# Reordering the attention-by-value units and the global rows' output in a fused local/global attention and MLP kernel

## Chip, cores and metric

One core of one Trainium2 chip. The metric is the device time of one execution in microseconds, with the median of all runs given. The kernel before takes 308.43 us (median of three runs, 307.68 to 312.75). The span in a profile (first to last instruction) is some 1.7 us shorter than that run's device time.

## The reference, cut to what matters

Batch 8, 8 heads, head width 64. Each batch has 32 global tokens, which attend to everything, and 512 local tokens, which attend to the 32 global ones and to their neighbours within 32 positions. The attention output of all heads is the input of an MLP with a quick GELU.

```python
# q_l, k_l, v_l: (8, 8, 512, 64)   q_g, k_g, v_g: (8, 8, 32, 64)
s_g  = scale * q_g @ concat(k_g, k_l).T          # global rows see all 544 tokens
out_g = softmax(s_g) @ concat(v_g, v_l)
s_ll = where(|i - j| <= 32, scale * q_l @ k_l.T, -1e9)
s_l  = concat(scale * q_l @ k_g.T, s_ll)         # local rows: 32 global keys + the window
out_l = softmax(s_l) @ concat(v_g, v_l)
x = concat(out_g, out_l).transpose(0, 2, 1, 3).reshape(8 * 544, 512)
h = x @ w_in                                     # 512 -> 2048
g = h * sigmoid(1.702 * h)
return g @ w_out                                 # 2048 -> 512, float32, 4352 rows
```

## The kernel before: the parts concerned

A `Quad` is four heads of one batch, so each batch has a first and a second head group. Scores are computed with keys on the partitions. The product with the values ("AV") is done in three *units*: unit 0 multiplies by ones and gives the denominators, units 1 and 2 give the two halves of the head width. Each unit fills one PSUM bank (a part of the memory that matmuls write their sums into; copying a finished bank out is its *eviction*) in two steps: `ekU` adds the global keys' share (four 32-row matmuls), and `U` adds the local keys' share (16 matmuls). Line numbers `L...` in the profiles are those of the kernel that ran.

```python
def XK(self, two=True):                 # exp of the global keys' scores, bank kb -> ek   (L375)
    nc.scalar.activation(self.ek, self.kb, AF.Exp, scale=scale)
    self.ek2 = None
    if two:                             # a copy turned by 32 partitions, by two transfers
        load_turned(nc.sync, self.ek2, self.ek)

def ekU(self, unit, warm=0, ov=None):   # a unit's global keys                             (L392)
    if ov is None:
        ov = pbank("ov")                # one of four PSUM banks, reused in turn
    ...
    two = unit == 1 and self.ek2 is not None   # unit 1 on the turned row group, beside unit 0
    ...

def ekUs(self, nxt=None, rnd=0, banks=(None, None, None)):   # all three, with the next keys between
    ...

def R(self):    # denominators: transpose sT (L442), reciprocal rT (L444), transpose rs (L446)
def XL(self, h):                        # xL = unit 1 + h times rs: frees that unit's bank (L451)
    nc.vector.tensor_mul(self.x[:, 2 * self.u + h, :], self.st[1 + h], self.st["rs"])
def Gm(self, og=None): ...              # the global queries' rows                         (L436)
def G(self):                            # ... scaled and transposed into xG                (L459)
    ...
    nc.vector.transpose(xG[:, 2 * self.u : 2 * self.u + 2, Sg * self.b : Sg * self.b + Sg], ...)

def o_mm(i, st): ...                    # output projection, op, four matmuls a step       (L512)
def o_out(i, tci, op):
    ...
    nc.scalar.activation(ob[:, lo:hi], op[:, lo:hi], AF.Copy, scale=0.5)       # eviction  (L526)
    for j in range(4):
        eng = nc.scalar if last and j % 2 else nc.sync
        ...
            r = (4 * tci + j) * S       # global tokens: batch-major, 32 rows per transfer
            rows = out[r : r + Sg, :]
        eng.dma_start(out=rows[:, lo:hi], in_=ob[32 * j : 32 * j + 32, lo:hi])

# batch 0, second head group c
for unit in range(3):
    c.ekU(unit)
for unit in range(3):
    c.U(unit)
c.R()
...
# batch 1: first head group a, second c
    a.XK(False)                         # no turned copy
    ...
    c.S(1)
    a.ekUs(c, 1)
    c.X(1)                              # exp of the scores (L339), then
    c.XK(False)                         # exp of the global keys
    for unit in range(3):
        a.U(unit)
    ...
    pt = spair()                        # the four banks of the scores c.S(1)
    a.Gm(bank(pt, 0)[:, 0 : D + 2])
    osteps(0, (3, 0), (3, 1))           # eight output matmuls
# the last batch, second head group
    for f4 in range(3):
        o_mm(i, 8 + f4)
    for unit in range(3):
        c.ekU(unit)
        c.U(unit)
    o_mm(i, 11)
    c.Gm()
    c.RXG()                             # R, XL(0), XL(1), G
    o(3)                                # takes the next PSUM bank in turn
```

The softmax here doesn't subtract the row's maximum and nothing guards it: scores larger than these inputs give would overflow.

## Time and profile before

From batch 2's second half on, the tensor engine's work repeats rigidly: two runs, laid over each other there, agree within a few hundredths of a microsecond until the last batch. So the span can be cut at fixed instructions into stretches, and a change shows in the stretch where it acts. The cuts are starts of matmuls on the tensor engine (PE), except the last two.

| stretch | from, to | before, us |
|---|---|---|
| start-up | start, to the second head group's first unit of batch 0 | 16.65 |
| batch 0 | to that group's global rows (L436) | 5.99 |
| MLP 0 | to the end of batch 1's scores (L327, at 47.05) | 24.41 |
| batch 1 | to the next keys' matmuls (L327, at 51.27) | 4.22 |
| middle | to the last batch's first unit (253.86) | 202.59 |
| last batch | to the first projection matmul after it (L487) | 6.95 |
| MLP 7 and globals | to the end of the last eviction on ScalarE (ACT) | 42.14 |
| tail | to the end of the span | 3.11 |

The timeline of PE in the kernel before, at batch 0, at batch 1 and at the last batch (start, duration, engine, line, operation, output and inputs, count; in brackets the idle time just before and what ended it):

```profile
16.88 0.88 PE L392 MATMUL ov<-ek,rvg 32*32 32x512 bf16 x8
17.68 0.49 PE L418 MATMUL ov<-e,ones 128*32 128x160 bf16 x16
...
18.94 1.67 PE L487 MATMUL s<-xL,w_in_sb 128*128 128x512 bf16 x7 [0.16 <-DMA w_in_sb<-in_moe_w_in_dram]
20.82 1.89 PE L487 MATMUL s<-xL,w_in_sb 128*128 128x512 bf16 x8 [0.21 <-DVE xL L451]
...
49.45 1.89 PE L512 MATMUL op<-w_out_sb,gT 128*128 128x512 bf16 x7 [0.34 <-ACT ek L375]
...
257.34 1.90 PE L512 MATMUL op<-w_out_sb,gT 128*128 128x512 bf16 x8
```

In batch 0 the eight global matmuls of units 1 and 2 take 0.88 us as one group, because the third unit waits for its bank inside it; the local units can only follow at 17.68. A bracket counts from the end of the last matmul, but in a running group the matmuls overlap: the seven from 18.94 start 0.216 us apart and last 0.38 us each. The last line has no bracket: PE did not wait there. The same place on VectorE (DVE):

```profile
254.72 0.72 DVE L442 STREAM_TRANSPOSE sT<-ov 128x512 f32<-128x512 f32 x1 [0.87 <-PE ov L418]
...
256.58 1.29 DVE L451 TENSOR_TENSOR xL<-ov,rs 128x512 bf16<-128x512 f32 x2
```

Two multiplies `xL` in 1.29 us: the first takes 0.69 us.

ACT at batch 1 in the kernel before, scores first, then the global keys:

```profile
47.16 1.66 ACT L339 ACTIVATE e<-s 128x856 bf16<-128x856 f32 x2
48.71 0.20 ACT L341 ACTIVATE e<-s 128x32 bf16<-128x32 f32 x1
48.79 0.62 ACT L375 ACTIVATE ek<-kb 128x512 bf16<-128x512 f32 x1
```

### The profile page before, as it was taken

Reading aid. Unit: us, or ns where it says so; the run is one execution under the profiler, and the core shown is the slowest. Engines: PE = TensorE matmul, PEld = TensorE weight load, DVE = VectorE, ACT = ScalarE, POOL = GpSimd, SP = SyncE. Lnnn points to the kernel's source line nnn. Section 1 sums busy time; section 2 is a strip of 40 time slices with the busy share of each in tenths; the row PEclk is TensorE's granted clock in tenths of the full one; section 3 lists DMA queues with packets and bytes.
Section 4 is the critical chain, followed back from the end, with each engine's and each line's share of the span. In section 5 each row is a group of like instructions: output and inputs, shape, how many; then the busy total and the mean of one; then the engine's idle time right before and its main releaser. Section 6 shows DMA issues by size and latency. Waiting matters only on the chain.

```text
span 306.1 us, 7822 instructions
## 1 busy us (share of the span) xinstructions
PE 296.3 (97%) x3230; PEld 148.3 (48%) x3265; DVE 211.0 (69%) x446; ACT 169.3 (55%) x282; POOL 54.4 (18%) x86
## 2 busy tenths in 40 slices
PE   7899999999999999999999999999999999999995
PEld 6454445444454455445454455445454454446653
DVE  6668847978957876777867876777777855574320
ACT  4828485485556745565556655565456661673421
POOL 8542755540050001400050002100000000000000
PEclk9999999999999999999999999999999999999999
DMA  7999999999399122951299023901230021201122
GB/s 192 180 208 206 191 150 224 211 176 145 79 98 181 33 56 71 149 110 28 62 116 174 3 57 85 106 0 40 51 79 9 2 62 38 60 0 35 37 61 77
DMA packets 56100, 29.39 MB, mean 96 GB/s; under 512 B 42880, under 2 KB 45952, under 8 KB 56064
## 3 DMA queue, kind: packets, MB, share of 16 engines
q0 software_dynamic: 45696, 16.95, 49.9%
q1 hardware_dynamic: 9888, 11.29, 14.2%
q10 hardware_dynamic: 480, 0.66, 0.6%
q8 instruction: 25, 0.41, 0.6%
q14 instruction: 11, 0.09, 0.1%
HBM read 35.13 MB, written 8.91 MB: 144 GB/s over the span
## 4 chain that ended last, share of the span: by engine, by line
PE 91%; ACT 3%; DMA 2%; DVE 1%; issue 1%; SPq 0%; ACTq 0%
PE op L512 38%; PE hp L487 37%; PE s L308 6%; PE ov L418 5%; PE ov L392 2%; DMA q<-in_q_l_dram 2%; ACT e L339 1%; PE kb L327 1%; PE op L524 1%; PE s L487 1%; PE s L327 1%; PE s L436 1%; ACT e L336 1%; DVE xL L451 0%; ACT ob L526 0%
## 5 line engine op out<-in xcount | busy, mean ns | idle before, releaser
L512 PE MATMUL op<-w_out_sb,gT 128*128 128x512 bf16 x504 | 120.0, 380 | 1.9 <-issue 0.5
L495 DVE SCALAR_TENSOR_TENSOR gT<-th,hp 128x512 bf16<-128x512 f32 (+1 forms) x140 | 91.2, 656 | 41.8 <-ACT th L494 40.7
L487 PE MATMUL hp<-xL,w_in_sb 128*128 128x512 bf16 x487 | 108.4, 379 | 0.6
L494 ACT ACTIVATE th<-hp 128x512 f32<-128x512 f32 (+1 forms) x140 | 79.8, 573 | 43.2 <-PE hp L487 39.7
L487 PEld LDWEIGHTS <-w_in_sb 128*128 128x128 bf16 x576 | 56.2, 98 | 64.8 <-issue 1.1
L512 PEld LDWEIGHTS <-gT 128*128 128x128 bf16 x528 | 49.3, 98 | 56.6 <-issue 3.8
L339 ACT ACTIVATE e<-s 128x856 bf16<-128x856 f32 x62 | 51.4, 882 | 12.1 <-PE s L436 7.0
L526 ACT ACTIVATE ob<-op 128x512 f32<-128x512 f32 (+2 forms) x35 | 20.5, 585 | 59.0 <-PE op L512 56.5
L89 POOL DMA_DIRECT2D v<-in_v_l_dram x24 | 18.7, 782 | 112.8 <-PE s L436 107.8
L442 DVE STREAM_TRANSPOSE sT<-ov 128x512 f32<-128x512 f32 x15 | 10.8, 717 | 27.1 <-PE ov L418 27.1
L346 DVE TENSOR_TENSOR e<-e,mask 128x1408 bf16<-128x1408 bf16 x28 | 24.4, 870 | 5.5 <-ACT e L339 5.5
L308 PE MATMUL s<-q,kT 32*128 32x228 bf16 (+5 forms) x528 | 21.2, 280 | 1.1 <-DVE q L269 1.1
L451 DVE TENSOR_TENSOR xL<-ov,rs 128x512 bf16<-128x512 f32 x30 | 19.4, 686 | 2.2 <-PE ov L418 0.9
L308 PEld LDWEIGHTS <-kT 32*128 32x128 bf16 x528 | 11.0, 95 | 14.9 <-issue 6.6
L265 DVE STREAM_TRANSPOSE kT<-rk 128x512 f32<-128x512 f32 (+1 forms) x17 | 16.9, 994 | 1.1 <-DMA rk<-in_k_l_dram 1.1
L375 ACT ACTIVATE ek<-kb 128x512 bf16<-128x512 f32 x16 | 9.7, 606 | 9.6 <-PE kb L327 9.6
L418 PE MATMUL ov<-e,v 128*32 128x160 bf16 (+1 forms) x480 | 12.1, 239 | 0.0
L446 DVE STREAM_TRANSPOSE rs<-rT 128x512 f32<-128x512 f32 x16 | 11.4, 711 | 0.6
L269 DVE STREAM_TRANSPOSE q<-rq 128x512 f32<-128x512 f32 (+1 forms) x17 | 10.9, 640 | 0.8 <-ACT rq L550 0.8
L418 PEld LDWEIGHTS <-v 128*32 128x32 bf16 x512 | 10.0, 97 | 0.9 <-issue 0.9
L327 PE MATMUL kb<-q,kgT 32*32 32x512 bf16 x128 | 10.1, 387 | 0.0
L487 PE MATMUL hp<-xG,w_in_sb 128*128 128x256 bf16 x64 | 9.6, 273 | 0.1
(80 smaller groups left out, 167.4 us busy)
## 6 DMA issues: line engine op xcount, KB each, us to landing
out_dram<-ob SPq DMA_DIRECT2D x132, 64.0 KB, 1.7
v<-in_v_l_dram POOLq DMA_DIRECT2D x32, 128.0 KB, 6.6
rq<-in_q_l_dram POOLq DMA_DIRECT2D x6, 512.0 KB, 8.7
rk<-in_k_l_dram POOLq DMA_DIRECT2D x6, 512.0 KB, 10.9
w_out_sb<-in_moe_w_out_dram POOLq DMA_DIRECT2D x4, 512.0 KB, 11.5
ek<-ek SPq DMA_DIRECT2D x12, 96.0 KB, 3.0
w_in_sb<-in_moe_w_in_dram POOLq DMA_DIRECT2D x4, 256.0 KB, 9.8
w_in_sb<-in_moe_w_in_dram POOLq DMA_DIRECT2D x2, 512.0 KB, 13.1
```

The costliest lines, as they stand in the source:

```text
L89: nc.gpsimd.dma_start(out=vtiles[b % 2][p, s, :, :, :D], in_=vf[b, g][:, hs])
L265: nc.vector.transpose(self.kT.rearrange("p (r t) -> p t r", t=16)[:, lo:hi], loaded[self.b][0][:, self.u].bitcast(F32)[:, 32 * lo : 32 * hi])
L308: nc.tensor.matmul(ps[j][:, off : off + n], lhsT=self.k[p, 128 * c : 128 * c + 128, e], rhs=self.q[p, lo:hi, r0 : r0 + nr, e], start=(e == ...
L339: nc.scalar.activation(e[:, 2 * i : 2 * i + 2, :RW], self.ps[i][:, :, :RW], AF.Exp, scale=scale)
L346: nc.vector.tensor_mul(e, e, mask[:, rnd : rnd + 1, :].to_broadcast([128, 4, LW]))
L418: nc.tensor.matmul(ov[32 * j : 32 * j + 32, :].rearrange("p (t r) -> p t r", t=16)[:, :, r0 : r0 + nr], lhsT=lv, rhs=self.E[c // 2][:, j, ...
L451: nc.vector.tensor_mul(self.x[:, 2 * self.u + h, :], self.st[1 + h], self.st["rs"])
L487: nc.tensor.matmul(hp[:, : width(i)], lhsT=w_in_c[:, fc // 8, kc, fc % 8 // 2, :, fc % 2], rhs=(xL[i] if i < B else xG)[:, kc, :], start=( ...
L494: nc.scalar.activation(th[:, :n], hp[:, :n], AF.Tanh, scale=0.851)
L495: nc.vector.scalar_tensor_tensor(gTs[i][:, fc, :n], in0=th[:, :n], scalar=1.0, in1=hp[:, :n], op0=ALU.add, op1=ALU.mult)
L512: nc.tensor.matmul(op, lhsT=gTs[i][:, fc, tci * 128 : tci * 128 + 128], rhs=w_out_sb[:, fc, :], start=(first and fc == 4 * f4), stop=(fc = ...
L526: nc.scalar.activation(ob[:, lo:hi], op[:, lo:hi], AF.Copy, scale=0.5)
```

## The change

Its intent: take PE's short waits out of batches 0 and 1, pack the last batch's units as the middle batches have them, and write the global tokens' output with fewer transfers. To do the last, the columns of `xG` are ordered by query first and batch second, so 128 rows of the output tile are 16 queries of all 8 batches, and two engines write half the columns each.

```diff
-                xG[:, 2 * self.u : 2 * self.u + 2, Sg * self.b : Sg * self.b + Sg],
+                xG.rearrange("p k (s b) -> p k s b", b=B)[:, 2 * self.u : 2 * self.u + 2, :, self.b],
@@ o_out
+            if i == B:
+                rows = out.rearrange("(b t) m -> t b m", t=S)[16 * tci : 16 * tci + 16]
+                mid = (lo + hi) // 2
+                nc.sync.dma_start(out=rows[:, :, lo:mid], in_=ob[:, lo:mid])
+                nc.scalar.dma_start(out=rows[:, :, mid:hi], in_=ob[:, mid:hi])
+                continue
             for j in range(4):
...
@@ batch 0
-    for unit in range(3):
-        c.ekU(unit)
-    for unit in range(3):
-        c.U(unit)
+    c.ekU(0)
+    c.ekU(1)
+    c.U(0)
     c.R()
+    c.U(1)
+    c.ekU(2)
+    c.U(2)
@@ batch 1
+    load_turned(nc.sync, rvt[:, 2:4], rvg[:, 2:4])
...
-    a.XK(False)
+    a.XK()
...
+    c.XK(False)
     c.X(1)
-    c.XK(False)
@@ last batch
+            c.ekUs()
             for unit in range(3):
-                c.ekU(unit)
                 c.U(unit)
```

(The change came under a title that also named "global values of batch 0 as f32"; the prediction refers to it.)

More of the change, by code (lines that the diff above doesn't have):

```diff
@@ L526, in o_out @@
             nc.scalar.activation(ob[:, lo:hi], op[:, lo:hi], AF.Copy, scale=0.5)
-            for j in range(4):
-                eng = nc.scalar if last and j % 2 else nc.sync
-                if i < B:
-                    rows = out[i * S + Sg : (i + 1) * S, :].rearrange("(r t) m -> t r m", t=16)[4 * tci + j]
-                else:
-                    r = (4 * tci + j) * S
-                    rows = out[r : r + Sg, :]
-                eng.dma_start(out=rows[:, lo:hi], in_=ob[32 * j : 32 * j + 32, lo:hi])
+            if i == B:
[4 more added lines that the diff above has]
+                continue
+            for j in range(4):
+                rows = out[i * S + Sg : (i + 1) * S, :].rearrange("(r t) m -> t r m", t=16)[4 * tci + j]
+                nc.sync.dma_start(out=rows[:, lo:hi], in_=ob[32 * j : 32 * j + 32, lo:hi])
     def act4(i, hf):
```

## The prediction

> **What bounds the kernel now.** I read the page's busy line and chain first, then the waits of the tensor engine alone, then the timeline at each place the diff touches.
>
> ```profile
> PE 296.3 (97%) x3230; PEld 148.3 (48%) x3265; DVE 211.0 (69%) x446; ACT 169.3 (55%) x282; POOL 54.4 (18%) x86
> ...
> PE   7899999999999999999999999999999999999995
> ...
> DMA  7999999999399122951299023901230021201122
> ...
> PE 91%; ACT 3%; DMA 2%; DVE 1%; issue 1%; SPq 0%; ACTq 0%
> ```
>
> PE is busy 296.3 of 306.1 us and carries 91% of the chain that ended last. The change takes no matmul away and adds none (3230 before; the built program has the same number), so it can only win idle time and badly packed time of PE, plus the two ends. The DMA row matters as well: nearly all slices up to about 46 us (6 of 40) stand at 9.
>
> ```profile
> PE op L512 <- ACT ek L375: 0.3, 1, 0.3
> PE s L487 <- DVE xL L451: 0.2, 1, 0.2
> ```
>
> These are two of the rows of the waits view for PE; no row there exceeds 1.5 us, and that one is the start-up. They are the waits the change is aimed at: 0.21 us in batch 0 (at 20.82) and 0.34 us in batch 1 (at 49.45). A change that wins both whole wins 0.55 us, 0.2% of the time. A third place shows in the timeline of PE, the last batch, where the units of AV run one by one:
>
> ```profile
> 253.86 0.39 PE L392 MATMUL ov<-ek,ones 32*32 32x512 bf16 x4
> 254.18 0.49 PE L418 MATMUL ov<-e,ones 128*32 128x160 bf16 x16
> 254.60 0.40 PE L392 MATMUL ov<-ek,rvt 32*32 32x512 bf16 x4
> 254.93 0.49 PE L418 MATMUL ov<-e,v 128*32 128x160 bf16 x16
> 255.34 0.40 PE L392 MATMUL ov<-ek,rvg 32*32 32x512 bf16 x4
> 255.67 0.49 PE L418 MATMUL ov<-e,v 128*32 128x160 bf16 x16
> 256.32 0.81 PE L512 MATMUL op<-w_out_sb,gT 128*128 128x512 bf16 x3 [0.16 <-issue]
> ```
>
> From 253.86 to 256.32 is 2.46 us. The same work in a middle batch stands packed:
>
> ```profile
> 85.06 0.40 PE L392 MATMUL ov<-ek,rvt 32*32 32x512 bf16 x4
> ...
> 85.63 0.49 PE L418 MATMUL ov<-e,ones 128*32 128x160 bf16 x16
> 85.95 0.78 PE L418 MATMUL ov<-e,v 128*32 128x160 bf16 x32
> 86.56 0.30 PE L436 MATMUL s<-v,e 128*32 128x66 bf16 x16
> ```
>
> There all global units begin at 85.05, the local ones at 85.63, and the next work at 86.56: 1.51 us, although eight matmuls for the next keys are mixed in.
>
> **What the Trainium skill says.** (1) "Perfetto Trace Analysis", Identifying the Most-Contended Engine: matmul busy share is no measure of the distance to the roofline, since pipelined instructions look different in the trace. It agrees here: in the last batch PE looks busy for all but 0.16 us of 2.46, yet the same work takes 1.51 elsewhere. (2) "TensorE: Matmul & The Clock Gate", Part 3: matmuls on different 32-row tiles run at once. It agrees: four 32x512 matmuls of 0.39 us each advance the chain by 0.33, and with values on a turned row group two units start 0.01 us apart (85.05 and 85.06). (3) "DMA: Bandwidth & Descriptors", Issuing engines are not separate DMA queues: transfers from all issuers interleave on the same 16 DMA engines. The trace agrees in landing times: an output write takes 1.7 us in the median of the whole kernel, 4.4 us when issued at 42 us among the loads. (4) Same page, Specifications: pieces under 512 B are below line rate. No line of before isolates it.
>
> **The change part by part.**
>
> *Global values of batch 0 as f32.* The title names it, but the diff has none of it; the kernel before already loads them so. 0.
>
> *Batch 0.* Before, the third global unit stands ahead of the first local one and waits for its bank until the multiply that ends at 17.31; local unit 0 starts at 17.68. After, it need not wait, so it starts near 17.25 (16.65 plus two global units) and the chain sT, rT, rs, eg, xL shifts by about 0.4 us; xL ends near 20.35 and PE needs it at 20.61. The wait of 0.21 goes. One more switch between global and local units costs perhaps 0.05. On PE: -0.15 to -0.2.
>
> *Does that last?* Not wholly. At 42 us DVE waits for a load, and PE's scores of batch 1 (44.04) follow directly:
>
> ```profile
> 42.23 1.05 DVE L265 STREAM_TRANSPOSE kT<-rk 128x512 f32<-128x512 f32 x1 [1.11 <-DMA rk<-in_k_l_dram]
> ...
> 43.73 0.42 DVE L279 COPY q<-qgT 128x40 f32<-128x40 f32 x4
> ```
>
> The first of these four copies ends near 43.9, so PE can come at most about 0.1 us earlier. And the change puts 49.5 KB (the turned values, rvt) and 128 KB (the turned exponentials, ek2) on the DMA engines in this crowded stretch. At some 190 GB/s, the page's rate there, 49.5 KB is 0.26 us; ek2 is issued only at 40.7. I put the delay of this load at 0.2 us. Batch 0 with this: +0.1.
>
> *Batch 1, turned values.* Packing as in the middle batches brings the local units from 47.85 to about 47.65 (0.80 us from the scores' end there, 0.63 in a middle batch): -0.2 if the data are there. ek2 needs its transfers landed at about 47.1. The exponential ends at 40.64, its two transfers are issued at 40.7 and 41.3. The like pair later:
>
> ```profile
> ek<-ek SPq DMA_DIRECT2D x1, 96.0 KB, 7.8
> ...
> ek<-ek SPq DMA_DIRECT2D x1, 32.0 KB, 7.5
> ```
>
> That was at 52 us, when output writes took 5.7 us; those issued at 42 us took 4.4. Scaled by 4.4/5.7 it is 6.0 and 5.8 us: landing at 46.7 and 47.1. A coin toss; I charge 0.2 us on average.
>
> *Batch 1, exp of global keys first.* The bank of kb is free sooner, so the 0.34 us wait goes. But the exp of the scores is now second on ACT, and the global-row matmuls (L436, 48.78 before) write into the pair of banks which that exp reads; in the built program they wait for its first half in both kernels. Before: the exp starts at 47.16 and its first half ends near 48.0, in time. After: kb is complete about 0.75 us after the scores (47.80, as 245.19 to 245.94 in a later batch), its exp takes 0.60, the first half of the other 0.86: 49.26. L436 starts at 49.3 instead of 48.78, and the output matmul at about 49.6 instead of 49.45: +0.15, and this swallows the packing's 0.2, which lies before the new wait. Batch 1 together: +0.35.
>
> *Last batch.* 253.86 + 0.58 (all global units, an upper bound since no next keys are mixed in) + 0.93 (local units) + 0.16 (switch) = 255.53 against 256.32: -0.8. ek2 already exists there, its bank waits are for an eviction that ended by 251.3, and what follows on DVE has over 2 us of slack. All of it is on PE's path and comes through to the end.
>
> *Global tokens in query-major order.* The little transposes (0.25 us each, off PE's path) write with a stride: at most 0.1 us each, hidden. The output goes in one transfer per queue instead of two:
>
> ```profile
> 301.71 0.38 ACTq L534
> ...
> 302.13 0.43 ACTq L534
> ...
> 302.61 0.33 ACT ob L526
> ```
>
> The second issue ends at 302.56 and the last matmul at 302.53, so the last eviction gains nothing. After it one issue of 0.43 instead of two: -0.4; but the transfer has 128 pieces of 384 B instead of 32 of 768 B, and issues with 96 rows took 0.53 to 0.61. I give half back: -0.2.
>
> Sum: +0.1 + 0.35 - 0.8 - 0.2 = -0.55 us.
>
> **The rivals.** (a) All aimed-at waits vanish and nothing takes their place: -0.2 - 0.5 - 0.8 - 0.4 = -1.9 us, about 306.5. For it: PE bound everywhere; against: the bank pair, fixed by the program's order. (b) ek2 or rvt lands late, since the DMA engines are full and the hardware queue shares with the loads: PE stands at the second global unit, and kb, both exps and L436 all move back with it, one for one. A landing 2 us later makes +1.5 us net, about 309.5. For it: 7.8 us of the like pair; against: 4.4 us of the writes at 42 us. (c) The strided small pieces at the end take longer than the saved issue: +0.5 us, 308.5. (d) The slow, unexplained executions (312.75 in the three runs of before) fall into the median: noise, not the change.
>
> **Range and chances.** Before: 308.43 in the median, 307.68 at best, and 307.79 in the profiled run; a typical run is thus near 308.2, and I take off 0.55: 307.6. Low 306.3 is rival (a) with a good draw; high 309.2 is (b) half true. 2% is 6.2 us, more than three times rival (a): faster 0.01, same 0.98, slower 0.01.
>
> **What would show it.** Right: the last batch's stretch shrinks to about 1.65 us; the wait of PE for xL is gone; PE shows a new wait at L436 near 49 us whose releaser is ACT; the ACT order there is ek before e. Wrong: a PE wait of over 0.5 us on the DMA of ek2 or rvt (rival b); L436 starts before 48.9 (my bank argument fell); the end of the last issue to the end of the span longer than in before by 0.4 us or more (rival c); DVE's wait for rk at 42 us unchanged (no extra load delay).

## The result

The changed kernel takes 308.37 us (median of six runs, 307.64 to 309.22); the kernel before took 308.19 in the median of its six. The ratio of the changed kernel to the one before is 1.0012, with a 95% interval of 0.9991 to 1.0034. Of the six of the kernel before, one (312.75) is 1.7% above the fastest and does not count as fast; the ratio leaves it out, the median does not. Here and below, a ratio is the mean time of one kernel's fast runs over the mean of the other's fast runs of the same rounds (in the experiments it comes out of the recorded times when each kernel's first, profiled run is left out), so it is not quite the ratio of the medians. So the time is the same: class and range of the prediction held, and the 0.55 us expected did not come.

The stretches of the two profiles:

| stretch | before | after | difference | predicted |
|---|---|---|---|---|
| start-up | 16.65 | 17.22 | +0.57 | 0 |
| batch 0 | 5.99 | 5.57 | -0.42 | -0.15 to -0.2 |
| MLP 0 | 24.41 | 24.42 | +0.01 | some +0.3 (later load, gain used up) |
| batch 1 | 4.22 | 4.28 | +0.06 | +0.35 |
| middle | 202.59 | 202.54 | -0.05 | 0 |
| last batch | 6.95 | 7.13 | +0.18 | -0.8 |
| MLP 7 and globals | 42.14 | 42.09 | -0.05 | 0 |
| tail | 3.11 | 3.36 | +0.25 | -0.2 |

The start-up is the same program in both, and it scatters between 16.65 and 17.92 over all 14 profiles, those of the kernel before included. Without it the differences sum to -0.02 us: the changed kernel gains 0.42 us in batch 0 and loses it again at the last batch and in the tail.

The waits view of PE of the changed kernel (engine, tile and line, releaser: total us, times, longest):

```profile
PE op L512 <- DVE xL L451: 0.8, 1, 0.8
PE s L436 <- ACT e L339: 0.4, 1, 0.4
```

Both of the waits aimed at are gone from this list, and two new ones stand in their place. The second was predicted; the first, the larger, was not. The timeline of PE at the three places (batch 0, batch 1, last batch):

```profile
17.76 0.49 PE L418 MATMUL ov<-e,ones 128*32 128x160 bf16 x16
...
18.49 0.40 PE L392 MATMUL ov<-ek,rvg 32*32 32x512 bf16 x4
...
19.24 3.63 PE L487 MATMUL s<-xL,w_in_sb 128*128 128x512 bf16 x16
...
49.38 0.32 PE L436 MATMUL s<-v,e 128*32 128x66 bf16 x16 [0.44 <-ACT e L339]
...
254.04 0.40 PE L392 MATMUL ov<-ek,rvt 32*32 32x512 bf16 x4
254.25 0.38 PE L392 MATMUL ov<-ek,rvg 32*32 32x512 bf16 x4
254.57 0.49 PE L418 MATMUL ov<-e,ones 128*32 128x160 bf16 x16
...
255.60 1.04 PE L512 MATMUL op<-w_out_sb,gT 128*128 128x512 bf16 x4
256.57 0.32 PE L436 MATMUL og<-v,e 128*32 128x66 bf16 x16
...
257.71 1.46 PE L512 MATMUL op<-w_out_sb,gT 128*128 128x512 bf16 x6 [0.80 <-DVE xL L451]
```

Batch 0: the third unit's global matmuls now stand at 18.49, and the 16 projection matmuls run as one group from 19.24, without the break of 0.21 us. Last batch: the units take 1.57 us (254.03 to 255.60; the prediction had 1.67 as an upper bound), but then PE stands for 0.80 us. DVE at the same place:

```profile
255.11 0.72 DVE L442 STREAM_TRANSPOSE sT<-ov 128x512 f32<-128x512 f32 x1 [1.08 <-PE ov L418]
...
256.97 1.29 DVE L451 TENSOR_TENSOR xL<-ov,rs 128x512 bf16<-128x512 f32 x2
```

The output matmul takes the next PSUM bank in turn, which is that of unit 1, and the first `xL` multiply, ending at 257.66, is what frees it. It is the same dependency as before, where it was met with 0.07 us to spare. With all global units ahead of the local ones, local unit 0 ends later, and `sT` starts 0.39 us later on the clock of each trace (255.11 against 254.72), 0.22 us later counted from the first unit; PE itself arrives 0.66 us earlier, counted likewise. Together this is the wait.

ACT at batch 1 in the changed kernel, now with the global keys first:

```profile
47.95 0.60 ACT L375 ACTIVATE ek<-kb 128x512 bf16<-128x512 f32 x1 [0.63 <-PE kb L327]
48.45 1.65 ACT L339 ACTIVATE e<-s 128x856 bf16<-128x856 f32 x2
```

The first half of the exp of the scores ends near 49.3, and L436, which writes into those banks, starts at 49.38 with PE idle for 0.44 us before it. The output transfers at the end (transfers view of a window around the last issues, 302.7 to 303.9 us, first of the kernel before, then of the changed one: output and input, queue, operation, count, KB each, median us from issue to landing):

```profile
out_dram<-ob ACTq DMA_DIRECT2D x2, 24.0 KB, 1.6
```

```profile
out_dram<-ob ACTq DMA_DIRECT2D x1, 48.0 KB, 2.2
```

One transfer of 48 KB instead of two of 24 KB is issued about 0.4 us before the second of those two, but it lands 2.2 us after its issue instead of 1.6.

### The profile page after: what moved, and what is told of

Its sections match the earlier page's. It is cut to its first block, busy times and chain, and to the rows that moved or that the text cites. A ratio compares the mean times of both kernels' runs of the same rounds, so it can differ in the third digit from the quotient of the medians.

```text
span 306.6 us, 7859 instructions
## 1 busy us (share of the span) xinstructions
PE 297.7 (97%) x3265; PEld 147.7 (48%) x3265; DVE 213.4 (70%) x446; ACT 169.4 (55%) x282; POOL 54.4 (18%) x86
## 4 chain that ended last, share of the span: by engine, by line
PE 82%; DVE 0%; ACT 0%; issue 0%
PE op L512 35%; PE hp L487 33%; PE s L308 5%; PE ov L418 4%; PE ov L392 2%; PE op L524 1%; PE s L436 1%; PE s L327 1%; PE s L418 0%; PE kb L327 0%; DVE xL L451 0%; DVE gT L495 0%; ACT th L494 0%; PE og L436 0%; PE s L392 0%; ACT ob L526 0%
## 5 line engine op out<-in xcount | busy, mean ns | idle before, releaser
L512 PE MATMUL op<-w_out_sb,gT 128*128 128x512 bf16 x528 | 121.9, 380 | 0.8 <-DVE xL L451 0.8
L512 PEld LDWEIGHTS <-gT 128*128 128x128 bf16 x528 | 49.3, 98 | 57.1 <-issue 4.3
L346 DVE TENSOR_TENSOR e<-e,mask 128x1408 bf16<-128x1408 bf16 x28 | 26.2, 936 | 6.6 <-ACT e L339 6.6
```

The costliest lines, as they stand in the source:

```text
L346: nc.vector.tensor_mul(e, e, mask[:, rnd : rnd + 1, :].to_broadcast([128, 4, LW]))
L512: nc.tensor.matmul(op, lhsT=gTs[i][:, fc, tci * 128 : tci * 128 + 128], rhs=w_out_sb[:, fc, :], start=(first and fc == 4 * f4), stop=(fc = ...
```

## Experiments

Each experiment starts from the changed kernel unless it says otherwise. One-look runs have one execution, of state unknown, at a clock of 0.998 to 1.000; I use them for their stretches, not for their time. All gave correct results. My theory at the start: the last batch's gain is lost to the bank that `xL` frees; batch 1 is bound by ACT in either order; the tail is lost to the pieces of the transfers.

### e1: the last batch's units one by one again

```diff
-            c.ekUs()
             for unit in range(3):
+                c.ekU(unit)
                 c.U(unit)
```

> The changed kernel with the last batch's units one by one again. In the changed kernel the output matmul after the global rows waits 0.80 us for DVE's xL; from the first global unit to the first projection matmul behind it takes 254.10 to 261.32 = 7.22 us, in the kernel before 253.93 to 260.97 = 7.04. Theory (the packed order meets the bank of AV unit 1 before DVE has read it, and the units packed ahead of local unit 0 delay that read): the wait of PE for xL is gone (under 0.1 us), the stretch is 7.04 +- 0.05. Rival (the wait comes from the output layout or slower transposes elsewhere, not from the packing): wait and 7.22 stay.

308.55 us, one run. The last batch takes 6.95 us, as in the kernel before; the wait for `xL` is gone, and all other stretches but the start-up stay as in the changed kernel within 0.15 us. So the +0.18 us belongs to this edit and to nothing else of the change.

### e2: the packed units in banks that nothing else is about to take

```diff
-            c.ekUs()
+            pt = spair()
+            c.ekUs(banks=[bank(pt, unit + 1) for unit in range(3)])
...
-            c.Gm()
+            c.Gm(bank(pt, 0)[:, 0 : D + 2])
```

> The changed kernel, last batch packed, but its three units and the global rows in the four banks of the score pair, which is free by then, so the next output matmul needs no bank that DVE still reads. Theory of the bank: the 0.80 us wait goes, the stretch from the first global unit to the first projection matmul falls from 7.22 to about 6.4 us (7.22 - 0.80, and the idle 0.05 beside it), the whole kernel by 0.8 us against the changed one. Rival (PE has to wait for xL at this place anyway, since the projection reads it): the wait moves to the projection matmuls, the stretch stays above 7.0.

307.69 us (median of six, 307.12 to 307.94) against 308.11 for the kernel before in the same rounds; the ratio is 0.9975, interval 0.9936 to 1.0015, widened by one run of the kernel before of 311.57. The last batch takes 6.28 us: 0.67 less than before, 0.85 less than in the changed kernel. PE there:

```profile
256.74 0.32 PE L436 MATMUL s<-v,e 128*32 128x66 bf16 x16
256.88 0.20 PE L436 MATMUL s<-rvg,eg 128*32 128x66 bf16 x4
257.02 1.47 PE L512 MATMUL op<-w_out_sb,gT 128*128 128x512 bf16 x6
```

The output matmul follows the global rows at once. The same order of instructions with other banks gives the gain back whole: the bank was the cause, and packing itself is worth 0.67 us. The medians differ by 0.42 us, and the profile, start-up left out, by 0.43, not 0.67: in this profile batch 2's queries came late (see r2), batch 1 took 4.36 us and the middle 202.91. The interval of the time includes 1.

### e3: the old layout of the global tokens and the old transfers

The edit puts the old `xG` columns and the old loop of `o_out` back (the first two parts of the diff above, reversed).

> The changed kernel with the old order of the global tokens and the old output transfers. In the changed kernel the transposes into xG take 0.47 us (0.25 before), a transfer issue at the end 0.54 to 0.65 (0.32 to 0.43), the last landing is 2.2 us after its issue (1.6), and from the end of the last eviction (303.25) to the end of the span is 3.35 us (before 302.94 to 306.1 = 3.16). Theory (128 small pieces per transfer are slower to issue and land by more than the second issue saved): transposes 0.25 us, tail 3.16 +- 0.08. Rival (the tail is noise of the run): tail of 3.35 or more.

309.42 us, one run. A miss: the tail came to 3.42 us, not to about 3.1, although its last transfers are those of the kernel before, piece for piece. Something else of the change reaches the tail. The trace shows what differs: after its last issue the sync engine (SP) checks nine semaphores one after another, each check some 0.06 us after the one before if its transfer has landed. In the kernel before, the transfer that lands last is met at the seventh of them, with two to follow; here it is met at the third, with six to follow. In the built programs the transfers of SP and ACT take eight semaphores in turn, and the change adds four transfers in batch 1, so each later one moved on by four. This became the theory that e9 tests.

The profile also caught two late loads: of batch 1's keys (DVE waits 1.62 us for them at 42.43 and PE 0.34 us at 44.13; MLP 0 took 24.82 us) and of batch 2's queries (see r2; batch 1 took 5.01 us).

### e4: batch 1's exps in the old order

```diff
-    c.XK(False)
     c.X(1)
+    c.XK(False)
```

> The changed kernel with the exp of the global keys of batch 1 behind that of the scores again, the turned values kept. From the scores' end (first 32x32 score matmul of the next global rows) to the next keys' matmuls: before 47.05 to 51.27 = 4.22 us, changed 47.21 to 51.49 = 4.28. Theory (ACT holds PE up in either order: the bank of kb in one, the pair of banks in the other, and the packing's 0.2 us lies ahead of both): the wait at L436 for ACT's e (0.44 us) is gone, a wait of the output matmul for ACT's ek of 0.4 to 0.6 us is back, the stretch 4.20 +- 0.06. Rival (the order of the two exps itself costs, so that the packing comes through once it is undone): 4.05 or less.

308.60 us, one run. Batch 1 takes 4.22 us, as in the kernel before, although its units are packed. Waits view of PE:

```profile
PE op L512 <- ACT ek L375: 0.5, 1, 0.5
```

The old wait is back, and longer than the 0.34 us of before by about what the packing had gained. ACT has both exps to do after the scores, whichever comes first, and PE waits for the second one in either order.

### e5: the global rows of batch 1 behind the eight output matmuls

```diff
-    a.Gm(bank(pt, 0)[:, 0 : D + 2])
     osteps(0, (3, 0), (3, 1))
+    a.Gm(bank(pt, 0)[:, 0 : D + 2])
```

> The changed kernel with the global rows of batch 1's first group (L436) moved behind the eight output matmuls that follow them, so that PE has work while ACT reads the pair of banks. Theory: neither order's wait is left, PE's wait at L436 under 0.05 us, the stretch from the scores' end to the next keys falls from 4.28 to about 3.85 us. Rival (what follows needs DVE's mask multiply of the later exp or another bank, and PE waits there): the stretch stays above 4.1, with a new PE wait of 0.3 us or more.

307.80 us, one run. The wait is gone and batch 1 takes 3.76 us, 0.52 less than in the changed kernel. The middle, however, grew by 0.29 us (202.83), so less than half of it remained (0.23 us); e10 shows where it goes.

### e6: batch 0 as before

The edit puts the two loops over the units of batch 0 back.

> The changed kernel with the old order of AV units in batch 0. From the first global unit of the second head group to its global rows: before 16.65 to 22.64 = 5.99 us, changed 17.22 to 22.80 = 5.58. Theory (the reorder is worth 0.41 us: two waits, for the bank and for xL, are both gone): 5.99 +- 0.05 and a PE wait for xL of about 0.2 us again. Rival (the weights' arrival, 0.58 us earlier relative to the work in the changed run, made the difference): stays below 5.7.

309.58 us, one run. Batch 0 takes 5.99 us and the break of 0.21 us before the projection matmuls is back, at 21.20. So the 0.42 us are the reordering's. This run too had the late load of the queries (batch 1 4.95 us, middle 202.91), which is why its time is no measure of the part.

### e7: the same two transfers, split by rows instead of columns

```diff
-                mid = (lo + hi) // 2
-                nc.sync.dma_start(out=rows[:, :, lo:mid], in_=ob[:, lo:mid])
-                nc.scalar.dma_start(out=rows[:, :, mid:hi], in_=ob[:, mid:hi])
+                nc.sync.dma_start(out=rows[0:8, :, lo:hi], in_=ob[0:64, lo:hi])
+                nc.scalar.dma_start(out=rows[8:16, :, lo:hi], in_=ob[64:128, lo:hi])
```

> The changed kernel with the last transfers split by rows instead of by columns: each queue takes 64 rows of 768 B (1280 B in the first piece) where the changed one takes 128 of 384 B (640 B). Theory of the pieces: half as many pieces, issue near 0.45 us and landing near 1.7 us, from the end of the last eviction to the end about 2.8 to 2.9 us, against 3.35. Rival (one transfer with two row dimensions is slow in itself, or fewer of the DMA engines take part since the outermost dimension is 8): 3.3 us or more.

308.94 us, one run. The tail is 3.99 us, 0.63 more than in the changed kernel, with 64 pieces of 768 bytes per transfer in place of 128 of 384. But this does not test the length of the pieces, for the trace bears out the rival named beforehand. In the changed kernel each of the last two transfers posts 16 landings on its semaphore, the last at 1.93 and 2.25 us after the last eviction; in e7 each posts one early and eight more, the last at 2.69 and 2.89 us. The outermost dimension of the new split is 8, so each transfer seems to have run on half of the 16 DMA engines. Whether the length or the count of the pieces made the changed kernel's transfers land late stays open.

### e8: the banks of e2, the order of e5 and the old rows of e3 together

> The changed kernel with three things mended: the bank pair in the last batch, the global rows of batch 1 later, the old token order and output transfers. If the three theories hold, and since they lie at three places of PE's path, 0.8 + 0.4 + 0.2 = 1.4 us less than the changed kernel and about 1.2 us less than before. Rival (later loads or evictions take it back): less than 0.5 us against before.

307.53 us (median of six; five from 306.97 to 307.65, one of 311.41 at a clock of 0.989); the ratio is 1.0002, interval 0.9961 to 1.0042, and it rests on that one run, which counts as fast. The stretches add as the single experiments had them: batch 1 3.76 us, last batch 6.28, middle 202.75, and a tail of 3.41, the tail of e3 again. Without the start-up this is 1.07 us less than before, not the 1.2 expected.

### e9: the kernel before, with four tiny transfers that nothing reads

```diff
+    spare = consts.tile([1, 4, D], F32)
+    for k in range(4):
+        nc.sync.dma_start(out=spare[:, k], in_=q_g[0, 0, k : k + 1, :])
     nq = {1: (Quad(2), Quad(3)), 2: (Quad(4), Quad(5))}
```

> The kernel before with four 256-byte transfers into a spare tile, issued by the sync engine where the change issues the turned values of batch 1; nothing reads them. If the closing checks of the sync engine go through the transfers' semaphores in turn, and the last landing transfer now has six of them behind it instead of two: tail 3.11 + 4 x 0.062 = 3.36, up to 3.42; all the rest as before. Rival (the tail follows from the pieces of the last transfers alone): tail 3.11 +-0.05.

309.22 us, one run. The tail is 3.40 us; every other stretch but the start-up (17.92 us) is that of the kernel before within 0.11 us. The sync engine's waits after its last issues, first the kernel before, then e9 (queue and line, releaser: total us, times, longest):

```profile
SPq L818 <- DMA out_dram<-ob: 0.9, 2, 0.6
```

```profile
SPq L821 <- DMA out_dram<-ob: 1.2, 1, 1.2
```

Before, SP stands twice, and some checks fall between the two landings, where they cost nothing. In e9 it stands once, at the semaphore of the last transfer, with six checks behind it. In the trace the check of that transfer is passed 2.09 us after the last eviction before and 2.13 in e9; after it come two checks before and six in e9, at steps of 0.06 us. Four times 0.061 and the 0.04 make 0.28 us, and the tail grew by 0.29. Four transfers of 256 bytes some 300 us earlier lengthen the end of the kernel. (SP ran them at 3.8 to 5.6 us, since they wait for nothing; what counts is that they come before the last ones in its order.)

In the changed kernel that check is passed at 2.27 us, with three to follow. Its +0.25 us is thus 0.18 of later landing and 0.06 of one more check. In e3 the landing was put right (2.15), but six checks followed.

### r1 and r2: the kernel before and the changed kernel again

> The kernel before again, for the scatter of the stretches: tail 3.11 +-0.05, last batch 6.95, batch 0 stretch 5.99, scores of batch 1 to next keys 4.22 unless the vector engine waits for a load of queries; the start-up anywhere from 16.6 to 17.6. If the stretches scatter by more than 0.1 us, the differences told for the parts are not to be believed.

> The changed kernel again: tail 3.35, last batch 7.13, batch 0 stretch 5.57, scores of batch 1 to next keys 4.28 unless the vector engine waits for a load of queries (then about 5.0, as in two of the experiments). Rival: the late load belongs to the change and shows here too.

308.59 us (r1) and 309.46 us (r2), one run each.

| stretch | before | r1 | after | r2 |
|---|---|---|---|---|
| start-up | 16.65 | 17.55 | 17.22 | 17.09 |
| batch 0 | 5.99 | 6.00 | 5.57 | 5.57 |
| MLP 0 | 24.41 | 24.41 | 24.42 | 24.66 |
| batch 1 | 4.22 | 4.22 | 4.28 | 4.94 |
| middle | 202.59 | 202.48 | 202.54 | 202.93 |
| last batch | 6.95 | 6.95 | 7.13 | 7.13 |
| MLP 7 and globals | 42.14 | 42.13 | 42.09 | 42.09 |
| tail | 3.11 | 3.14 | 3.36 | 3.33 |

The stretches repeat within 0.03 us but for the middle (0.11) and, in r2, three stretches in a row. In batch 1 the timeline of DVE has

```profile
51.37 0.71 DVE L269 STREAM_TRANSPOSE q<-rq 128x512 f32<-128x512 f32 x1 [1.13 <-DMA rq<-in_q_l_dram]
```

DVE waits for batch 2's queries and PE then for DVE (0.59 us at 52.26), which costs r2 0.66 us in batch 1 and goes on into the middle (0.39). The 0.24 us in MLP 0 come earlier, from batch 1's keys: DVE waits 1.28 us for them at 42.42, and PE 0.18 us at 44.31. Together it is 1.3 us against the first profile of the same program. The wait for the queries (0.56 to 1.21 us) stands in 4 of the 10 profiles that have the turned values of batch 1, and in none of the 4 without. The loads there hint at the same: the 48 KB load of global values issued at 40 to 41 us lands after 5.5 to 5.6 us in the four without, after 5.4 to 6.9 us (mean 6.15) in the ten with. Four in ten against none in four can be chance. The landing times of the load of the queries itself, issued at 42.1 to 43.6 us, leave less room for it: 6.1 to 6.7 us (mean 6.4) in the four without, 6.8 to 8.2 (mean 7.4) in the ten with, so each of the ten is slower than each of the four. e10, which has the new orders of batches 0 and 1 but not the turned values, is among the four. So the turned values go with a load about 1 us later; whether DVE has to wait for it differs from run to run. No experiment adds the turned values alone.

### e10: the best of the parts, with the order of transfers as before

Against the kernel before, the layout and transfers of the end and the turned values are left as they were. Batch 0 is that of the change. The rest is:

```diff
@@ batch 1
-    c.X(1)
     c.XK(False)
+    c.X(1)
...
-    a.Gm(bank(pt, 0)[:, 0 : D + 2])
     osteps(0, (3, 0), (3, 1))
+    a.Gm(bank(pt, 0)[:, 0 : D + 2])
@@ last batch
+            pt = spair()
+            c.ekUs(banks=[bank(pt, unit + 1) for unit in range(3)])
             for unit in range(3):
-                c.ekU(unit)
                 c.U(unit)
             o_mm(i, 11)
-            c.Gm()
+            c.Gm(bank(pt, 0)[:, 0 : D + 2])
```

> The changed kernel with three things put otherwise: the last batch's global units in the score pair's four banks, batch 1's global-row matmuls behind the eight output matmuls, and the old output rows and no turned values for batch 1, so that the order of all transfers is that of before. If the stretches add and the tail depends on the order of the transfers: batch 0 stretch 5.57, scores of batch 1 to next keys about 3.93 (3.76 plus the 0.17 of packing that is given up), last batch 6.28, tail 3.11 (+-0.06), so apart from the start-up 1.3 to 1.4 us less than before. Rival (the tail does not depend on the order of the transfers): tail 3.3 to 3.4, total 1.0 to 1.1 us less than before. Rival (gains are eaten up by waits later): middle stretch over 202.9.

307.17 us (median of five, 306.74 to 307.68) against 307.87 of the kernel before (nine runs, 307.73 to 308.45). The ratio is 0.9977, interval 0.9964 to 0.9991: a small gain, about 0.7 us, far below 2%, but the only one here whose interval leaves out 1. Batch 0 is 5.57 us, batch 1 3.94, last batch 6.28 and tail 3.13, all as expected, so the tail depends on the order of the transfers. The middle is 202.76, where r1 has 202.48. Without the start-up the sum is 1.1 us less than r1, not the 1.3 to 1.4 expected. The difference is the middle: in the trace two successive projection matmuls of batch 1, at 4.57 us after the next keys, start 0.52 us apart where 0.21 is usual. The `xL` multiply before the second of them ends there. DVE's own chain began no earlier (its `xL` multiplies of the first head group start 4.64 us after the end of batch 1's scores, 4.63 in r1), so the 0.28 us that PE had won in batch 1 is lost a few microseconds later.

## Why the prediction was right or wrong

**Batch 0: right in kind, twice as large.** I priced the wait for `xL` at its bracket, 0.21 us. From start to start it cost 0.37 us (20.24 to 20.82, where 0.216 is usual), and the change won that whole. The units won only 0.05 us: from the first of them to the first projection matmul it was 2.07 us before (with the unrecorded matmul at 18.72) and is 2.02 now. The third unit no longer waits for its bank, but its later place costs nearly as much.

**The delay of the load at 42 us: absent in these two profiles.** MLP 0 is 24.41 and 24.42, so neither the extra load delay nor a gain used up there appeared, and in the changed profile DVE does not wait for that load at all. In six of the ten profiles with the turned values it does (0.19 to 1.62 us), and in two of these, r2 and e3, MLP 0 is 0.24 and 0.40 us longer. The load itself took 8.1 to 8.6 us (mean 8.33) in the ten and 8.1 to 8.3 (mean 8.20) in the four without: a delay within the scatter. The larger one, about 1 us, fell on the next load, batch 2's queries, of which the prediction says nothing. It also took the turned values for 49.5 KB; the two transfers carry 24.8 and 8.2 KB.

**Batch 1: the mechanism was right, the sum too high.** The new wait of L436 for ACT stands at 49.38, predicted 49.3. Rival (b), late turned values, cost nothing. Only in e6 do they come late (the second transfer lands at 47.78 us, and inside unit 1 a matmul starts 0.33 us after the one before); this moves the local units by 0.1 us and is swallowed by the wait for ACT. That takes the charge of 0.2 us away, and the prediction's +0.15 proved to be +0.06.

**The last batch: the failed step.** The prediction said that "its bank waits are for an eviction that ended by 251.3, and what follows on DVE has over 2 us of slack". The first half is about the units' own banks. The second is false for the output matmul behind them, which needs unit 1's bank back; the slack was 0.07 us. In its place the runs showed a new wait of 0.80 us (changed kernel), none with other banks (e2) and none in the old order (e1). The size was off as well: the row at 256.32 that I took for the end of the old units has x3 where four matmuls ran, and the unrecorded first one was PE working, not waiting for 0.16 us. (The trace records 3230 matmuls; both built programs have 3265, and not 3230 as the prediction says.) The true start is near 256.09 and the gain to be had 0.67 us, not 0.8.

**The tail: wrong in sign.** The prediction gave -0.2 for one issue less. The larger transfer ate up the 0.4 us that its earlier issue had saved and 0.18 us beyond (landed 2.27 against 2.09 us after the last eviction). A second term was in no step of mine: the place of the last transfer among SP's closing checks, +0.06 us in the change and 0.24 of the 0.29 us in e9. Rival (c), slow strided small pieces, had the direction, with twice the size (+0.5 us); whether small pieces are the reason no run isolates.

**The strided transposes: wrong in size, and harmless.** They take 0.47 us each instead of 0.25, where I allowed 0.1 us more; no wait of PE follows from them.

**The whole.** My -0.55 us was the sum of four terms (batch 0 with the load, batch 1, last batch, the end), each off by 0.3 to 1.0 us: two came out better and two worse than predicted, and what was left of the errors, 0.5 us, happened to lie inside the range. What was sound is the bound: a change that leaves the matmuls as they are, in a kernel whose PE is busy for 97% of the span, can win only from gaps and bad packing, so the range was narrow and same was nearly certain.

## What to carry to other kernels

Before moving work forward on a busy engine, list what the *following* instructions need and when it was ready, also where no wait shows: a dependency met by 0.07 us is the next bottleneck, and here another bank removed it (e2). Measure a wait of PE from start to start: here a bracket of 0.21 us had cost 0.37, and 0.16 us in brackets was a matmul missing from the trace. A part put back for an experiment carries side effects with it, as the order of the transfers did in e3, so check the other stretches before reading the total. Cut the trace at fixed instructions and compare stretch by stretch; the start-up alone scattered by 1.3 us here, more than all parts of the change together.

## What the Trainium skill lacked or had wrong

- "Advanced Engine Details and Errata", Network/Comms, gives 50 to 100 ns for a sequencer to read a semaphore; SP's closing checks follow each other in about 60 ns, which agrees. What no page has is that the order of these checks counts: with the same final transfers, the tail was 3.11 us with two checks behind the last landing and 3.40 us with six.
- "DMA: Bandwidth & Descriptors", Specifications, gives 512 bytes as the least transfer for line rate. No run here isolates it: transfers of 128 pieces of 384 bytes ended with a tail of 3.36 us and those of 64 pieces of 768 bytes with 3.99 us, but the latter posted 8 landings each in place of 16.
- No page has the price in time of a strided output for the small transpose on DVE: 128x64 bf16 took 0.47 us instead of 0.25.
- None that I used warns of a dependency that is met just in time and leaves no gap to be found: 0.07 us of slack in the kernel before became a wait of 0.80 us.
